# Three pieces of an attention front end: their queries loaded as squares and transposed by VectorE, in place of rows transposed by TensorE

## The chip, the cores and the metric

One core of one Trainium2 chip. The metric is the device time of one execution in us, as the median of several executions. Differences here are of 1 to 5 us in 1028, so means of many runs and 95% intervals matter, and so does each run's mean granted TensorE clock (1.000 is full speed).

## The reference, cut to what matters

```python
scores = scale * np.matmul(q, k.transpose(0, 1, 3, 2))        # q, k, v: (8, 8, 576, 64) fp32
ret    = scores * Dmat                                         # causal, decaying by head
x      = np.matmul(ret, v)  ->  (4608, 512)
h      = x @ w_in                                              # 512 -> 2048
g      = h * erf(softplus(h))
out    = g @ w_out                                             # 2048 -> 512
```

The attention is computed in 36 pieces of 128 tokens. The two large products follow and take nearly all the time.

## The kernel before: the parts concerned

Both operands of the scores have the head dimension on the partitions, so each piece of q and k is transposed. There are two ways to do it. A piece loaded as rows (two DMAs of 128 KB, runs of 256 B) is transposed by TensorE (PE) in four instructions into PSUM, and ScalarE copies it out. A piece loaded as squares of 32 x 32 (four DMAs of 112 KB, runs of 896 B) is transposed in one instruction by VectorE (DVE) into SBUF. Here q is in rows for pieces 0 to 7 and in squares from 8 on.

```python
SQUARES = 2 * PC                 # PC = 4: pieces 0 to 7 of q are rows
...
for name in names:               # load(i, names)
    if name == "q" and i < SQUARES:
        t["q"] = load_rows(i, "q", q, 2)
    elif name == "q":
        t["qs"] = load_squares(i, "q", q)
...
def transposes(i):
    ...
    for name in "qk":
        if name + "s" in t:
            nc.vector.transpose(out=tT..., in_=squares...)              # L322
        else:
            nc.tensor.transpose(pt[:, p, :], ..., ident)  x4            # L328
            nc.scalar.copy(out=tT..., in_=pt...)
    load(i + 2, "q")
def outputs(i):
    ...
    load(i + 3, "kv")
...
# the front part; a: next attention stage, p: next plain product of the first chunk,
# w: load weights, 5: five steps of rounding a weight block on DVE
for what in "alkakakawkakakawaa3awwa2aaa5ppappawwppa5ppapp5wawcppa5ppappaa5s":
```

Where a stage stands in that string fixes what each of its instructions stands behind on its engine. The trace of after shows it: the transpose of piece 6 started on DVE at 51.13 us, right behind the rounding step before it (L271), although its squares had all landed at 43.61.

## Time and profile before

| | before |
|---|---|
| median of 6 runs | 1027.55 us (1027.11 to 1028.71) |
| span of the profiled run, clock | 1026.0 us, 0.999 |
| PE busy | 1017.5 us, 99% |
| DVE busy | 669.1 us, 65%, but 9.46 of 10 us between 40 and 50 us |

PE is the bound over the whole, but before 60 us it works in turn with DVE and the loads. The prediction shows the lines. What is missing there is the list of PE's waits (engine, line, what ended the wait: us in all, times, longest). These are three of its five lines for the kernel before; the other two are 1.4 us at the very start and 0.8 us for a state that GpSimd (POOL) makes:

```profile
PE pt_k L328 <- DMA raw_k<-in_k_dram: 0.7, 2, 0.4
PE p L546 <- DVE wa L271: 0.7, 1, 0.7
PE s L343 <- DVE kT L322: 0.2, 1, 0.2
```

No wait of PE on the changed path reaches 1 us. The trace of before also has what the two ways cost: one of PE's 128x128 transposes takes 273 ns (median), but four, overlapping, take 0.44 us of the chain (46.39 to 46.83); DVE transposes a piece of q of 128x512 in 699 ns (median), 24 times, and ScalarE copies only the eight pieces that are in rows (586 ns each). SyncE's loads take turns on eight semaphores there (100 to 107), each after the landing of the one eight places before: the load of raw_v at 27.40 us was issued right after the one of 20.06 had landed at 27.34.

### The profile page before, as it was taken

To read this page: it belongs to the slowest core of one execution; us is meant where nothing else is said; L and a number is where in the kernel's file an instruction comes from. 1 tells how busy PE (TensorE), PEld (TensorE's weight loads), DVE (VectorE), ACT (ScalarE), POOL (GpSimd) and SP (SyncE) were. 2 spreads that over 40 slices of the span, in tenths; PEclk is the share of its full clock that TensorE was granted. 3 is DMA by queue.
4 is the path that set the end of the run, shared out by engine and by line. 5 is a ranking of instruction groups with operands and counts; after the bars stand their busy time and mean duration, and the time that the engine had idled before them with its cause. 6 is when DMAs were issued, how large, how long until landed. Compare 5 with 4: busy or idle time off the path is not lost.

```text
span 1026.0 us, 15946 instructions
## 1 busy us (share of the span) xinstructions
PE 1017.5 (99%) x6346; PEld 876.1 (85%) x6346; DVE 669.1 (65%) x1054; ACT 390.4 (38%) x481; POOL 123.7 (12%) x122
## 2 busy tenths in 40 slices
PE   9999999999999999999999999999999999999998
PEld 8778888888888888888888888888888888888887
DVE  3868777877976656656666666666567655555555
ACT  2254134233234444434343444444433333333332
POOL 2143112122312110010001001000100000000000
PEclk9999999999999999999999999999999999999999
DMA  9999889979984344544444345444333334444333
GB/s 197 191 241 194 224 194 221 251 155 248 242 187 161 120 150 145 168 158 163 156 150 163 123 146 160 167 144 144 144 124 124 123 131 126 131 136 133 124 91 115
DMA packets 146986, 165.76 MB, mean 162 GB/s; under 512 B 97376, under 2 KB 121568, under 8 KB 138848
## 3 DMA queue, kind: packets, MB, share of 16 engines
q1 hardware_dynamic: 145904, 163.96, 56.5%
q8 instruction: 50, 0.82, 0.3%
q10 hardware_dynamic: 1008, 0.79, 0.3%
q14 instruction: 24, 0.20, 0.1%
HBM read 117.52 MB, written 47.19 MB: 161 GB/s over the span
## 4 chain that ended last, share of the span: by engine, by line
PE 89%; DMA 5%; DVE 3%; SPq 3%; issue 1%; POOL 0%; DVEq 0%; POOLq 0%
PE a L600 23%; PE a L492 22%; PE g L600 11%; PE g L492 11%; PE e L600 6%; PE e L492 5%; PE s L343 3%; PE o L361 2%; DMA raw_qs<-in_q_dram 1%; PE p L546 1%; SPq L145 1%; PE o L384 1%; PE o L372 1%; DMA raw_k<-in_k_dram 1%; SPq L131 1%; DMA raw_ks<-in_k_dram 1%
## 5 line engine op out<-in xcount | busy, mean ns | idle before, releaser
L492 PE MATMUL a<-x,wa 128*128 128x256 f32 x1088 | 258.3, 380 | 0.0
L492 PEld LDWEIGHTS a<-x,wa 128*128 128x128 f32 x1088 | 205.7, 190 | 28.5
L600 PE MATMUL a<-wb,s 128*128 128x256 f32 x864 | 205.7, 381 | 0.0
L600 PEld LDWEIGHTS a<-wb,s 128*128 128x128 f32 x864 | 162.9, 190 | 23.6 <-ACT o L614 0.7
L99 DVE TENSOR_TENSOR t<-g,t 128x512 f32<-128x512 f32 x68 | 46.9, 690 | 150.3 <-ACT t L522 113.1
L492 PE MATMUL g<-x,wa 128*128 128x256 f32 x544 | 129.2, 380 | 0.0
L492 PEld LDWEIGHTS g<-x,wa 128*128 128x128 f32 x544 | 102.8, 190 | 14.4
L99 DVE TENSOR_TENSOR o<-a,o 128x512 f32<-128x512 f32 x108 | 74.2, 687 | 49.3 <-PE a L600 49.3
L517 ACT COPY t<-a 128x512 f32<-128x512 f32 x34 | 19.9, 586 | 188.2 <-PE a L492 188.2
L99 DVE TENSOR_TENSOR t<-t,s 128x1024 f32<-128x1024 f32 x72 | 89.6, 1285 | 0.0
L561 ACT ACTIVATE s<-t 128x1024 f32<-128x1024 f32 x72 | 72.1, 1049 | 27.8 <-DVE t L99 27.8
L270 POOL TENSOR_TENSOR wraw<-wraw 128x512 f32<-128x512 f32 x28 | 29.5, 1053 | 435.6 <-DVE wraw L268 178.9
L99 DVE TENSOR_TENSOR x<-x 128x512 f32<-128x512 f32 x115 | 75.8, 692 | 1.2
L528 ACT COPY t<-a 128x512 f32<-128x512 f32 x34 | 19.9, 587 | 144.4 <-PE a L492 144.4
L565 ACT ACTIVATE s<-s 128x1024 f32<-128x1024 f32 x72 | 72.1, 1049 | 0.4
L600 PE MATMUL g<-wb,s 128*128 128x256 f32 x288 | 68.6, 381 | 0.0
L600 PE MATMUL e<-wb,t 128*128 128x256 f32 x288 | 68.5, 380 | 0.0
L600 PE MATMUL a<-wb,t 128*128 128x256 f32 x288 | 68.5, 380 | 0.0
L600 PE MATMUL g<-wb,t 128*128 128x256 f32 x288 | 68.2, 380 | 0.0
L99 DVE TENSOR_TENSOR sT<-s,cst 128x512 f32<-128x512 f32 x72 | 46.2, 682 | 32.5 <-PE s L343 32.5
L99 DVE TENSOR_TENSOR o<-g,o 128x512 f32<-128x512 f32 x72 | 49.3, 684 | 24.6 <-ACT o L614 19.8
L492 PE MATMUL e<-x,wa 128*128 128x256 f32 x272 | 64.8, 381 | 0.0
(75 smaller groups left out, 1226.2 us busy)
## 6 DMA issues: line engine op xcount, KB each, us to landing
od<-o SPq DMA_DIRECT2D x54, 512.0 KB, 3.3
x<-xd SPq DMA_DIRECT2D x27, 1024.0 KB, 4.8
o<-od SPq DMA_DIRECT2D x27, 1024.0 KB, 5.2
raw_qs<-in_q_dram SPq DMA_DIRECT2D x96, 112.0 KB, 4.4
raw_ks<-in_k_dram SPq DMA_DIRECT2D x84, 112.0 KB, 4.1
xd<-x SPq DMA_DIRECT2D x9, 1024.0 KB, 5.3
raw_k<-in_k_dram SPq DMA_DIRECT2D x64, 128.0 KB, 4.5
raw_v<-in_v_dram SPq DMA_DIRECT2D x64, 128.0 KB, 4.5
```

What stands on the lines that cost most here:

```text
L99: nc.vector.tensor_tensor(out=out, in0=in0, in1=in1, op=op)
L131: nc.sync.dma_start(out=t[part * SQ : (part + 1) * SQ, :, at : at + m - SQ], in_=tokens[:, :, d0 : d0 + m - SQ])
L145: nc.sync.dma_start(out=t[r0 : r0 + n, e::2, :], in_=heads.rearrange("h p d -> p h d"))
L270: engine.tensor_tensor(out=r_f, in0=high_f, in1=r_f, op=ALU.mult)
L343: nc.tensor.matmul(ps[e][:, p, :], lhsT=t["kT"][heads[e], p, :], rhs=t["qT"][heads[e], p, :], start=True, stop=True)
L361: nc.tensor.matmul(o[p % 2][heads[(e + p) % 2], p // 2, :], lhsT=t["v"][:, 2 * p + e, :], rhs=t["sT"][:, e, p, :], start=(p < 2), stop=(no ...
L492: nc.tensor.matmul(acc[:, j * TH : (j + 1) * TH], lhsT=weights["wa", self.g][:, a, d, j * P : (j + 1) * P], rhs=x[self.g, self.c][a][:, d, :],
L517: nc.scalar.copy(out=self.t1[:, 1], in_=self.a)
L528: nc.scalar.copy(out=self.t2[:, 0], in_=self.a)
L561: nc.scalar.activation(self.s[:, j], t, AF.Softplus)
L565: nc.scalar.activation(self.s[:, j], self.s[:, j], AF.Erf)
L600: nc.tensor.matmul(acc[:, tp, :], lhsT=left[:, j * TH + tp * P : j * TH + (tp + 1) * P], rhs=weights["wb", self.g][:, b, j, :], start=(sta ...
```

## The change

Its intent: PE is 99% busy and DVE 65%, so move query transposes from PE to DVE. It does so for pieces 5, 6 and 7 (the sixth to eighth).

```diff
-    SQUARES = 2 * PC
+    SQUARES_Q = PC + 1
...
-                if name == "q" and i < SQUARES:
+                if name == "q" and i < SQUARES_Q:
...
-        if i < SQUARES:
+        if i < 2 * PC:
             weigh_values(i)
...
-        if i + 1 >= SQUARES:
+        if i + 1 >= 2 * PC:
             weigh_values(i + 1)
```

The last two edits keep the scaling of the values where it was.

## The prediction

> **What bounds the kernel now.** I read the page first: the busy times, then the slices. The first number after an engine is its busy time in us, in brackets the share of the span.
>
> ```profile
> PE 1017.5 (99%) x6346; PEld 876.1 (85%) x6346; DVE 669.1 (65%) x1054; ACT 390.4 (38%) x481; POOL 123.7 (12%) x122
> PE   9999999999999999999999999999999999999998
> DVE  3868777877976656656666666666567655555555
> DMA  9999889979984344544444345444333334444333
> ```
>
> TensorE (PE) is the bound nearly everywhere. But the slices show another kernel in front: in the first 60 us DMA and VectorE (DVE) are as full as PE. I therefore asked for busy time by stretch (columns: stretch, its length, then busy us and instructions of each engine, clock, DMA share, GB/s).
>
> ```profile
> 0.00:20.00 20.00, 18.18 (x194) 16.61 (x194) 4.93 (x10) 4.70 (x7) 4.28 (x10) 1.00 0.95 192
> 40.00:60.00 20.00, 18.31 (x197) 14.97 (x196) 15.91 (x30) 11.63 (x19) 5.71 (x6) 1.00 0.87 193
> 40.00:50.00 10.00, 9.28 (x95) 7.51 (x93) 9.46 (x17) 2.85 (x5) 1.80 (x2) 1.00 0.96 206
> 80.00:1020.00 940.00, 939.78 (x5533) 811.51 (x5528) 617.02 (x959) 359.69 (x434) 100.78 (x94) 1.00 0.54 158
> ```
>
> From 80 us on PE idles 940.00 - 939.78 = 0.2 us. So whatever PE loses or gains before 80 us should move the end by as much, and nothing later gives it back. Between 40 and 50 us DVE is at 9.46 of 10: there DVE, not PE, sets the pace. All three changed pieces fall in just this front part: the transposes of their queries on PE start at 31.61, 46.23 and 51.85 us. The chain of waits (start us, us, what) says what PE waits for there:
>
> ```profile
> 26.32 6.20 DMA raw_k<-in_k_dram
> 32.52 0.14 issue
> 32.65 0.63 PE pt_k L328 x4
> ...
> 38.42 1.14 PE s L343 x16
> 39.56 1.27 DVE sT L99 x2
> ...
> 43.65 0.70 DVE wa L271
> 44.35 0.04 issue
> 44.40 1.99 PE p L546 x8
> 46.39 0.44 PE pt_q L328 x4
> 46.83 0.44 PE pt_k L328 x4
> ```
>
> So the path goes from a DMA (keys of the sixth piece, landing at 32.52) through PE to DVE (mask of the scores, then six steps rounding a weight block) and back to PE's first product, which idles 0.72 us for them.
>
> [...]
>
> **The change part by part.**
>
> *Removed from PE:* per piece four transposes, 0.44 us of PE time when their input is there (46.39 to 46.83). Three pieces: 1.3 us, the whole upside. *Removed from ScalarE:* three copies of 0.59 us; ScalarE is at 38% and these are not on the path, so 0.
>
> *Added to DVE:* three transposes of 0.70 us, about 0.65 us each in a dense row; 2.0 us in all, where DVE is full.
>
> *Loads.* Per piece two row DMAs of 128 KB become four square DMAs of 112 KB (448 KB for 256 KB, since the rows overlap). In a dense stream row DMAs land about 0.52 us apart: the two of q and the two of k of the sixth piece are issued at 23.81, 25.22, 25.77 and 26.32 and take 7.14, 6.25, 6.22 and 6.20 us, landing at 30.95, 31.47, 31.99, 32.52. Square DMAs land 0.47 to 0.67 us apart: those issued at 88.75, 89.13, 89.60 and 90.08 take 2.5, 2.6, 2.7 and 2.9 us. I take 0.46 for squares. So per piece 4 x 0.46 - 2 x 0.52 = +0.8 us of DMA time ahead of the keys, in spite of the larger runs. The number of DMAs matters too: each issue waits for the landing of the one eight places before it (the order of instructions shows eight semaphores in rotation), so the keys' DMAs move two places and issue at about 27.4 and 28.4 in place of 25.8 and 26.3. That is still some 5 us before they would land, so I charge nothing for it.
>
> *Moved:* the order of instructions is the point that the diff does not show. On DVE, in order, the sixth piece's transpose stands behind the second weight block's rounding and before the state of the fifth piece: harmless, the squares are there at 32.3 and DVE passes there at about 35. The seventh piece's transpose stands **behind** the last step (L271) of the fourth weight block; the scores of that piece on PE must now wait for it. In before, PE did these scores while DVE was still rounding:
>
> ```profile
> 48.92 1.16 PE L343 MATMUL s<-qT,kT 64*128 64x128 f32 x16
> 49.25 0.69 DVE L271 TENSOR_TENSOR wa<-wa,wraw 128x512 f32<-128x512 f32 x1
> 50.02 1.99 PE L546 MATMUL p<-x,wa 128*128 128x256 f32 x8
> ```
>
> The scores start 1.0 us before L271 ends (49.94) and the products that need L271 follow without a gap. In after it must be L271, transpose, scores, products, one after the other. The eighth piece's transpose comes behind four rounding steps well before its scores: hidden.
>
> *Sum, replayed with the durations above.* Step 1: keys of piece six land at 32.52 + 0.84 = 33.4; their transposes on PE end at 34.1 in place of 33.28: **+0.85**, although the query transposes there are gone (PE simply waits about 1.9 us from 31.55). Everything to L271 of the fourth block moves with it: scores, mask, third block, products at 45.3, fourth block, L271 end at 50.8. The third block's load has 0.85 us of slack of its own (landed 39.13, DVE takes it up at 40.75 because of the mask), and the step before it has moved by the same, so it does not bind. The removed query transposes of piece seven (0.44) only lengthen the wait. Step 2: 50.8 + 0.67 transpose = 51.5; scores 1.09, so the products start at 52.6 in place of 50.02: **another +1.75**. Step 3: piece eight has no query transposes on PE: **-0.44**. Sum +0.85 + 1.75 - 0.44 = +2.2 us. From there to 59.3 us the chain alternates PE and DVE as before and is only shifted, and after that PE is full. 1027.58 + 2.2 = 1029.8.
>
> **Rivals.** (a) *The bound engine simply loses work:* -1.3 us, 1026.3. For it: PE 99% and the engine taking the work at 65%. Against it: those are averages over 1026 us; in the 30 us concerned DVE is at 95% and PE waits. (b) *Larger runs relieve the DMA:* keys arrive earlier. If they landed by 31.6, PE would save about 1.2 us there, and with step 2 and 3 the sum is about 0: 1027.6. For it: [...] 512 packets in place of 1024, and SP's issues being held up to 4.9 us in this stretch with rows. Against: the landing intervals measured above. (c) *The wait moves on:* the extra DMA time of 0.8 us per piece delays a weight block beyond its slack, or later pieces' squares: up to 2 us more, 1031.8. For it: DMA is at 0.87 to 1.05 to 60 us. Against: the seventh and eighth pieces' keys have over 1 us of slack in the replay. (d) *The two new PE gaps (about 1.9 and 2.2 us) cool the clock:* 2 us or more on top; [...] unlikely.
>
> **Range and chances.** The three steps are known to some tenths each; the least sure is step 1 (0 to +1.5), next the length of the fourth block's rounding, which took 4.7 us where the third took 3.6 while GpSimd worked beside it. I hold rival (b) at one in six, (a) at one in twelve, (c) at one in six. That gives 1029.8, with 1027.0 to 1031.6 for 8 in 10. All rivals together stay within 0.5%, and 2% is 20 us, so "within 2%" at 0.985; faster 0.005, slower 0.01 (a slip in the order that I do not see).
>
> **What would show it.** Right: PE's 16 scores of the seventh piece start just after a DVE transpose that starts just after L271 of the fourth block, with a PE gap of about 2 us before them; the keys of the sixth piece land near 33.4 and PE waits for them; PE still full after 80 us; PE busy about 1.3 us less, span 2 us more. Step 1 is wrong if those keys land before 32.5; step 2 if the scores start before L271 ends or the gap is under 1 us. The whole is wrong if PE is idle less than before ahead of 60 us, or if PE shows gaps after 80 us.

## The result, and the profile after

| | before | after |
|---|---|---|
| median of 6 runs | 1027.55 us | 1033.18 us (1030.1 to 1036.5) |
| span of the profiled run, clock | 1026.0 us, 0.999 | 1031.2 us, 0.998 |
| PE busy | 1017.5 us | 1016.9 us |
| DVE busy | 669.1 us | 670.5 us |

The ratio of fast runs is 1.0054 [1.0034, 1.0074]. Ratios here are the mean time of one kernel's fast runs over that of the other's of the same rounds, so not quite the ratio of the medians quoted. By the 2% rule it is "same", but the time lies above the predicted range, and the runs spread over 6 us where those of before spread over 1.6.

The page of after, busy times and three rows of slices:

```profile
PE 1016.9 (99%) x6334; PEld 875.3 (85%) x6334; DVE 670.5 (65%) x1057; ACT 389.1 (38%) x478; POOL 122.6 (12%) x122
PE   8899999999999999999999999999999999999998
DVE  3868877877876666666566666666667655555555
DMA  9997979979984444444445344444433334444333
```

The averages hardly moved, and PE is busy less than before while the kernel is longer. So look at stretches (length, busy us and instructions of PE, PEld, DVE, ACT, POOL, then clock, DMA share, GB/s):

```profile
40.00:60.00 20.00, 17.12 (x147) 13.71 (x148) 14.32 (x25) 6.47 (x11) 5.12 (x5) 0.91 0.98 207
80.00:1020.00 940.00, 938.62 (x5538) 810.34 (x5537) 619.48 (x963) 360.77 (x436) 100.82 (x94) 1.00 0.54 157
```

PE did no more than 17.12 of 20 us there (18.31 before) at a clock of 0.91; after 80 us it idles 1.4 us in 940 (0.2 before). PE's waits in after:

```profile
PE pt_k L328 <- DMA raw_k<-in_k_dram: 2.6, 2, 2.0
PE s L343 <- DVE qT L322: 2.2, 1, 2.2
PE s L343 <- DVE kT L322: 1.4, 1, 1.4
```

The first two are steps 1 and 2 of the prediction, in name and nearly in size. The third lies at 240 us and is taken up below. The chain of waits shows step 2 in full, and one thing more:

```profile
50.52 0.04 DVE wa L271
...
51.13 0.71 DVE qT L322
51.85 0.14 issue
51.98 1.16 PE s L343 x16
53.14 3.40 PE p L546 x8
56.54 0.65 PE pt_k L328 x4
```

The last rounding step, the transpose, the scores and the products now come one after the other, as predicted. But the eight products took 3.40 us; the same eight took 1.99 us at 50.02 in the kernel before (the prediction shows that line). Busy time by windows between the changes of the granted clock tells why (columns as above; third from the end is the clock):

```profile
50.02:53.43 3.41, 1.45 (x18) 1.33 (x19) 2.07 (x4) 1.01 (x2) 0.00 (x0) 1.00 1.00 342
53.43:56.84 3.41, 3.41 (x11) 2.68 (x10) 3.31 (x7) 1.07 (x3) 0.29 (x1) 0.50 0.51 112
56.84:60.25 3.41, 3.41 (x39) 2.75 (x41) 0.19 (x1) 2.80 (x6) 3.04 (x3) 1.00 0.85 242
```

After a window in which PE was busy 1.45 of 3.41 us, the clock was 0.50 for the whole next window, then 1.00 again. Half a window of work is lost: 3.41 x 0.50, about 1.7 us.

To locate gains and losses I compared the start of the same instruction in two traces: of the scores of piece 5 (after step 1), 6 (after step 2) and 7 (after step 3), which the prediction calls the sixth, seventh and eighth piece, and the end. Us later than in the first profile of before:

| profile | clock falls | piece 5 | piece 6 | piece 7 | first output product (84 us) | end |
|---|---|---|---|---|---|---|
| predicted | 0 | +0.85 | +2.6 | +2.2 | +2.2 | +2.2 |
| after, first | 1 | +1.27 | +3.06 | +4.31 | +3.99 | +5.26 |
| before, again (two looks) | 0 | -0.07, +0.44 | -0.07, +0.44 | -0.07, +0.44 | -0.39, +0.13 | +0.64, +0.96 |

All three steps are there, plus a fall of the clock in the products between pieces 6 and 7 (+1.7), plus 1.3 us late. The theory after this: the three steps are right, and the pause that step 2 makes on PE pulls its clock down in some executions, depending on how it lies against windows of 3.41 us; that is the excess and the spread. Rivals: the loads land later than the sum has it; or late waits for key squares have grown.

### The profile page after: what moved, and what is told of

Same layout as the page of the kernel before. It is cut to its first block, busy times and chain, and to the rows that moved or that the text cites. A ratio compares the mean times of both kernels' runs of the same rounds, so it can differ in the third digit from the quotient of the medians.

```text
span 1031.2 us, 15926 instructions
## 1 busy us (share of the span) xinstructions
PE 1016.9 (99%) x6334; PEld 875.3 (85%) x6334; DVE 670.5 (65%) x1057; ACT 389.1 (38%) x478; POOL 122.6 (12%) x122
## 4 chain that ended last, share of the span: by engine, by line
PE 92%; DMA 4%; SPq 2%; DVE 1%; issue 0%; DVEq 0%
PE a L600 24%; PE a L492 22%; PE g L600 12%; PE g L492 11%; PE e L600 6%; PE e L492 6%; PE s L343 3%; PE o L361 3%; PE o L384 1%; PE o L372 1%; DMA raw_k<-in_k_dram 1%; DMA wraw<-in_moe_w_in_dram 1%; DMA raw_qs<-in_q_dram 1%; PE p L546 1%; SPq L145 1%; SPq L131 1%
```

## The experiments

All gave correct results. Edits are against the changed kernel, shortened.

### One piece at a time

```diff
-                if name == "q" and i < SQUARES_Q:
+                if name == "q" and i < 2 * PC and i != 5:     # only_sixth; 6: only_seventh; 7: only_eighth
```

> Only the sixth piece's queries as squares; seventh and eighth as rows. Theory A (the predicted chain, plus a clock that falls when TensorE idles for most of one of the throttle's windows of 3.41 us): step 1 alone. Keys of the sixth piece land about 0.8 us later than in the kernel before, TensorE waits about 2 us for them, the scores of the seventh piece again run before the last rounding step L271 ends. Without a fall of the clock 1028.4 us; runs with a fall 1.0 to 1.7 us more. Rival B (the excess over the prediction comes from later waits for loads, in the stretch of 100 to 300 us, and has nothing to do with the clock): 1028.4 plus 1 to 2 us at a mean clock as before, with a wait of over 1 us after 100 us in the profile.

> Only the seventh piece's queries as squares. Theory A: step 2 alone. The scores of the seventh piece wait for the transpose that waits for L271 of the fourth block: TensorE gap of about 1.6 us (rows of the sixth piece leave TensorE less idle before), products at L271 end + 0.7 + 1.1 us. Without a fall of the clock 1029.3 us, with one 1030.5 to 1031. No long wait for the sixth piece's keys. Rival B: 1029.3 plus 1 to 2 us at an unchanged clock, wait after 100 us.

> Only the eighth piece's queries as squares. Theory A: step 3 alone, four TensorE transposes gone and nothing waits for the VectorE transpose: 1027.1 us, 0.4 below the kernel before; no TensorE gap over 1 us after 5 us, clock as before (0.999), runs within 1 us of each other. If squares cost TensorE by themselves, or DMA time in this stretch binds (rival B), it is at or above the kernel before.

| run | median (range), runs | ratio to before | piece 5 | piece 6 | piece 7 | end | runs with clock 0.998 or less |
|---|---|---|---|---|---|---|---|
| only_sixth | 1029.87 (1027.89 to 1031.94), 13 | 1.0013 [1.0005, 1.0021] | +1.34 | +1.34 | +1.34 | +2.36 | 1 |
| only_seventh | 1031.37 (1029.27 to 1031.94), 10 | 1.0024 [1.0015, 1.0033] | +0.35 | +2.15 | +2.15 | +2.61 | 3 |
| only_eighth | 1028.97 (1027.57 to 1033.93), 14 | 1.0006 [0.9995, 1.0017] | +0.68 | +0.69 | +0.25 | +1.20 | 2 |

(Before on the same chip: 1028.56, 1027.19 to 1030.08, 32 runs, none under 0.999.) Steps 2 and 3 are in the profiles by themselves: 2.15 - 0.35 = +1.80 for the seventh, 0.25 - 0.69 = -0.44 for the eighth. The sixth's +1.34 is not step 1 alone: its piece 4, which the change does not touch, was already at +1.46, and only_seventh and only_eighth, which load piece 5 as rows, are at +0.35 and +0.68. The step is sized below. Against the expectations the times missed upwards: +1.3, +2.4 and +0.7 us over the mean of before, where +0.9, +1.8 (without a fall) and -0.4 were expected. The clock does not account for all of that: the seven runs of only_seventh at 1.000 are 2.2 us above before, on the mean. The sum of the ratios' excesses is 0.43%, close to the 0.44 to 0.54% of the whole. In the profile the eighth's gain is not banked: PE then waits 1.2 us for the keys of the tenth piece.

### Filling the pauses of PE with work that nothing needs

If the clock falls because PE is idle, products of the identity in the pause should keep it up, at no cost as long as they end before the operands come. They are in front of the scores of piece 6 (fill_gap), and in fill_both, fill_little and fill_pair also in front of the key transposes of piece 5.

```diff
     def scores(i):
         ...
+        if i == 6:
+            for _ in range(18):     # fill_both, fill_pair: 8; fill_little: 3
+                nc.tensor.matmul(ps[0][:, 0, :], lhsT=ident, rhs=ident, start=True, stop=True)
     def transposes(i):              # not in fill_gap
         ...
+        if i == 5:
+            for _ in range(8):      # fill_little: 3
+                nc.tensor.matmul(pt[:, 0, :], lhsT=ident, rhs=ident, start=True, stop=True)
```

> The changed kernel with 18 useless transposes' worth of matmuls (identity by identity, into a PSUM place that the scores overwrite) on TensorE just before the seventh piece's scores, where it idled 2.15 us. Theory A: the path is the same, TensorE is merely busy in the gap, so the clock no longer falls: mean clock 0.999 in nearly all runs, 1030.0 to 1031.2 us, spread under 1.5 us (the gap before the sixth piece's keys of 2.0 us is still there, and may let the clock fall in some run). Rival B: no change, 1033 us with runs from 1030 to 1036.

> The changed kernel itself once more, on the chip of the next three runs, for comparison. Theory A (chain of +2.2 us, plus windows of 3.41 us at half the clock that come when TensorE idles for most of one): median 1032 to 1034.5 us, run times falling together with the mean clock, which lies between 0.995 and 0.999. Theory C (the excess over +2.2 is only the unsteady landing of early and later loads, as the 3 us of spread in the kernel before on this kind of chip would suggest): the same times, but unrelated to the clock.

> The changed kernel with 8 useless products of the identity (0.23 us each at fp32, as the earlier filling run showed: 18 took 4.18 us, too long for the gap) in each of the two TensorE gaps: before the sixth piece's key transposes and before the seventh piece's scores. About 1.9 us of filling for gaps of 2.0 and 2.15 us. Theory A: mean clock 0.999 to 1.0 in all runs, median 1030 to 1031.3 us, no run over 1033. Theory C: median as that of the changed kernel in this call, within 0.5 us.

> The changed kernel with only 3 useless products (0.7 us) at the start of each of the two TensorE gaps, which leaves gaps of about 1.3 and 1.4 us. Theory A, sharpened: in the ten profiles so far the clock fell after those windows of its 3.41 us grid in which TensorE idled 1.97 and 2.01 us, and after none with 1.73 us or less. So two gaps under 1.5 us cannot lower it: clock 0.999 to 1.0 in all runs, 1030 to 1031.5 us, as with the longer filling. If instead any gap of over 1 us can do it, the clock is 0.998 or less in half of the runs and the median 1032 to 1033.

fill_gap missed: 1034.39 (1031.51 to 1038.26, 6 runs), ratio 1.0065 [1.005, 1.008], slower than the change itself. The 18 products took 4.18 us for a pause of 2.2, so the scores started late by the difference, and three of six runs still were at 0.998 or less. The other pause, before the keys of piece 5, had been left open; that it is the reason is not shown, since none of the three was profiled. With both pauses filled and fewer products:

| run | median (range), runs | ratio to before | clocks of the runs |
|---|---|---|---|
| after_again | 1032.42 (1030.09 to 1033.32), 5 | 1.0044 [1.0031, 1.0057] | 1.000, 0.998 x3, 0.997 |
| fill_both, same chip | 1030.91 (1030.0 to 1032.39), 5 | 1.0032 [1.002, 1.0045] | 1.000 x3, 0.999 x2 |
| fill_little, another chip | 1031.5 (1029.53 to 1034.05), 13 | 1.0029 [1.0021, 1.0038] | 1.000 x8, 0.999 x5 |

No run of these filled kernels fell under 0.999, which shows that the pauses pull the clock down. It does not settle the times: at clocks of 0.999 or 1.000 fill_both is still 3.2 us and fill_little 2.9 us above the mean of before, and the 13 runs of fill_little spread over 4.5 us. Three products in each pause were enough to hold the clock at 0.999 or more in all 13 runs; PE's timeline of fill_little (start us, us, what, in brackets the wait):

```profile
49.79 0.83 PE L346 MATMUL s<-ident 128*128 128x128 f32 x6
52.11 1.16 PE L349 MATMUL s<-qT,kT 64*128 64x128 f32 x16 [1.49 <-DVE qT L322]
53.20 1.99 PE L552 MATMUL p<-x,wa 128*128 128x256 f32 x8
```

(The three products are six records.) The pause is cut from 2.2 to 1.49 us and the eight products take 1.99 us. The time gained is 1.2 us on the means of the pair on one chip, with overlapping intervals, so it was tried again at the end (below).

### Taking away the cause of each step

transpose_early moves the transpose of piece 6 ahead of the fourth weight block's rounding; early_and_keys_first also loads the keys of pieces 5 to 7 before their queries.

```diff
-    for what in "...ppapp5wawcppa5...":
+    for what in "...ppappe5wawcppa5...":       # e: early_q(6), DVE's transpose of the loaded squares
```
```diff
-        load(i + 2, "q")                        # in transposes
+        if i + 2 not in (5, 6, 7):
+            load(i + 2, "q")
...
-        load(i + 3, "kv")                       # in outputs
+        if i + 3 in (5, 6, 7): load k, then q, then v of i + 3
+        else: load(i + 3, "kv")
```

> The changed kernel with the seventh piece's VectorE transpose put ahead of the fourth block's rounding, the only change. Step 2 of the chain then costs 0.65 us (the transpose itself on VectorE) in place of 1.75: the scores run beside the rounding again, TensorE waits for L271 with its products for about 0.6 us. With step 1 +0.85 and step 3 -0.44: +1.1 us over the kernel before. Theory A: one of the two long gaps is gone, so fewer falls of the clock: in all +1.1 to +2.5 us. If step 2 was not the cause, it is as slow as the changed kernel.

> The same, and the keys of the sixth to eighth piece are loaded ahead of their squares of queries. Step 1 then falls away: the sixth piece's keys land at about 31.9 us, their transposes on TensorE start without a long wait, and the whole runs at -0.8 (step 1 turned round) + 0.65 - 0.44 = -0.6 us: at or up to 1 us below the kernel before, no TensorE gap over 1.2 us, clock as in the kernel before, so no slow runs. If squares bind by their DMA time itself and not by standing ahead of the keys, it is no faster than the run with the early transpose alone.

transpose_early: 1029.66 (1028.7 to 1032.33, 8 runs), ratio 1.0024 [1.0013, 1.0034]. Its timeline has the old order again:

```profile
49.09 1.16 PE L351 MATMUL s<-qT,kT 64*128 64x128 f32 x16
50.13 0.69 DVE L271 TENSOR_TENSOR wa<-wa,wraw 128x512 f32<-128x512 f32 x1
50.88 1.99 PE L554 MATMUL p<-x,wa 128*128 128x256 f32 x8 [0.62 <-DVE wa L271]
```

The scores start before the rounding ends, piece 6 is at +0.17, where the five profiles of the changed kernel have +2.33 to +4.59, and the end at +0.95. That settles step 2's cause. Two of eight runs still were at 0.998; the first pause was still there.

early_and_keys_first missed: 1031.19 (1029.48 to 1034.92, 9 runs), ratio 1.0035 [1.0022, 1.0048], where a gain was expected. In its profile pieces 6 and 7 did start 1.07 and 0.84 us *earlier* than in before. That gain was lost twice: 1.4 us in a wait for the tenth piece's keys, and later PE waited 2.5 us for key squares and its clock fell at 237.94 us, after a window with 2.01 us idle. The likely reading is that loads moved ahead push other loads back; for the tenth piece's keys the next runs bear it out, for the wait near 240 us nothing tests it.

### Can the eighth's gain be banked?

The keys of the tenth piece are put ahead of its queries, with only the eighth piece changed (eighth_keys_ahead), without any change (before_keys_ahead, an edit of the kernel before), and together with all of the above (all_ahead). As in the edit above, transposes then leaves those queries out.

```diff
+        if i + 3 in (9,): load k, then q, then v      # all_ahead: (5, 6, 7, 9), and early_q(6)
```

> Only the eighth piece as squares, and the tenth piece's keys loaded ahead of its query squares. Theory A': the 0.44 us of step 3 were lost again at the tenth piece, whose keys TensorE then waited for (1.2 us in the profile of the run with the eighth piece alone). With those keys about 2 us earlier the gain stays: 0.3 to 0.5 us below the kernel before, if the run below of the order alone gains nothing. Rival: the saving is lost elsewhere, same as the kernel before.

> The kernel before with the tenth piece's keys loaded ahead of its query squares, the only change: separates the order from the squares. TensorE reaches that place at about the moment when the keys land (67.86 and 67.84 us), so at most 0.1 to 0.3 us faster; same within noise.

> The changed kernel with the early VectorE transpose of the seventh piece, the keys of the sixth to eighth piece ahead of their squares, and the tenth piece's keys ahead too. The run without the last part was 0.84 us ahead of the kernel before at 64 us and lost 1.4 us to the tenth piece's keys. Now that wait is gone: first product of the second half of the block at 83.6 to 84.0 us in place of 84.49, and with clocks of 1.0 about 0.5 to 0.8 us below the kernel before in the middle of its runs. If the loads as a whole bind (squares take more DMA time than rows), the wait moves to the next load and it is no faster than the kernel before.

| run | median (range), runs | ratio to before |
|---|---|---|
| eighth_keys_ahead | 1029.05 (1027.79 to 1030.58), 13 | 1.0003 [0.9995, 1.0011] |
| before_keys_ahead | 1028.28 (1027.67 to 1030.54), 13 | 0.9998 [0.999, 1.0007] |
| all_ahead | 1031.26 (1029.53 to 1033.2), 13 | 1.0022 [1.0014, 1.0031] |

In the profile of eighth_keys_ahead the wait for the tenth piece's keys is gone and the first output product starts 0.21 us earlier than in the first profile of before. But two other profiles of before lie at -0.39 and +0.13 there, and the times show no gain. all_ahead missed: its front is level with before (+0.04 at 84 us), yet it ends +3.0 us late, with 2.4 us of waits for key squares. No version tried beats the kernel before.

### Two more looks at each kernel

> The kernel before, one more profile. Asked: how long TensorE waits for the key squares (VectorE's transpose of them) between 205 and 285 us, 0.2 us in its first profile. Theory D (the change makes this late wait longer): 0 to 0.5 us here and 0.5 to 2.6 in the profiles of the changed kernel. Theory E (it is unsteady landing that both share): 0 to 1.5 us in both. No window with over 1.5 us of TensorE idle, no fall of the clock.

> The kernel before, as in the first look: theory D 0 to 0.5 us of late wait, theory E 0 to 1.5 us; no fall of the clock.

> The changed kernel, one more profile. Theory D: late wait 0.5 to 2.6 us. Theory E: 0 to 1.5 as in the kernel before. For the clock: a fall to half for 3.41 us comes after each window of the grid with over about 1.9 us of TensorE idle and after none with under 1.7; up to 53 us the delay is +2.2 us plus 1.7 for each fall.

> The changed kernel, as in its first look: theory D 0.5 to 2.6 us of late wait, theory E 0 to 1.5 us; falls of the clock after windows with over about 1.9 us of TensorE idle and no others.

Single runs (state unknown) on one chip: before 1028.38 and 1028.74, after 1035.39 (clock 0.997) and 1030.36 (clock 1.000). The late waits for key squares were 0.8 and 0.9 us in before, 2.1 and 1.1 us in after: before missed theory D's 0 to 0.5, and 2.1 is over theory E's 1.5, so neither stands as it was put. The rule for the clock held: at piece 7 after_look1, with two falls, is at +5.84 us (2.2 + 2 x 1.7 = 5.6 expected), after_look2, with none, at +1.89 (2.2). The two profiles of after are the same program, 5.0 us apart, and show the cause best. The pause before the scores of piece 6 in the good one, PE's timeline:

```profile
51.26 1.16 PE L343 MATMUL s<-qT,kT 64*128 64x128 f32 x16 [2.20 <-DVE qT L322]
52.35 1.99 PE L546 MATMUL p<-x,wa 128*128 128x256 f32 x8
```

and its two clock windows around it:

```profile
49.70:53.11 3.41, 1.85 (x20) 1.69 (x21) 2.06 (x5) 1.23 (x2) 0.00 (x0) 1.00 1.10 317
53.11:56.52 3.41, 3.41 (x20) 2.75 (x20) 3.10 (x7) 2.25 (x4) 0.69 (x1) 1.00 0.71 106
```

The pause is the same 2.2 us as in the first profile of after (2.15), but a boundary at 49.70 cuts it, so the window holds 1.56 us of idling and the clock stays. In the bad one both pauses lie within a window, and both are followed by half speed:

```profile
30.89:34.30 3.41, 1.09 (x8) 0.72 (x7) 2.66 (x5) 1.07 (x2) 0.00 (x0) 1.00 0.86 170
34.30:37.72 3.42, 3.42 (x9) 2.25 (x8) 1.32 (x3) 0.59 (x1) 1.04 (x1) 0.50 0.77 192
51.37:54.78 3.41, 1.27 (x17) 1.18 (x18) 2.06 (x4) 1.23 (x2) 0.00 (x0) 1.00 0.96 235
54.78:58.19 3.41, 3.41 (x9) 2.59 (x10) 3.31 (x7) 0.58 (x1) 0.11 (x1) 0.50 0.81 206
```

### The pair once more

> The changed kernel once more, five rounds, on the same chip and in the same call as fill_pair. Theory (the pause pulls TensorE's clock down in most executions): most of its runs have a mean clock of 0.998 or less, those are at 1032 to 1036 us, and the runs at 0.999 or 1.0 are at 1030 to 1030.5; mean about 1032.5. Rival (the excess over the predicted +2.2 us is late loads, not the clock): the times do not sort by the clock.

> The changed kernel with 8 identity products in each of the two pauses, once more, on the same chip as after_pair. Theory: no run under 0.999, and the mean is 1 to 2 us under that of after_pair, near 1031, since the three serial steps (+2.2 us) and 0.2 us of products that overrun stay. Rival: same mean as after_pair within 0.5 us, since the work is the same and the products do nothing.

On one chip in one call (before 1028.33, 11 runs): after_pair 1033.52 (1030.97 to 1035.86, 6 runs), ratio 1.0052 [1.0038, 1.0065]; fill_pair 1032.36 (1031.46 to 1032.58, 5 runs), ratio 1.0039 [1.0027, 1.0051]. Five of the six runs of after_pair were at 0.998 or 0.997 and took 1032.85 or more; the one at 0.999 took 1030.97. No run of fill_pair was under 0.999. Its mean is 1.25 us lower, as in the first pair (1.2), again with overlapping intervals, and not quite near 1031: in its profile the keys of piece 5 landed only at 34.35 us (33.84 in the first profile of after), and the products of the identity held PE from 32.85 to 34.63 us, some 0.3 us past that, so that the scores of piece 5 were 1.95 us late. A fixed filling does not fit a pause whose length varies.

The 17 timed fast runs of the changed kernel (first result, after_again, after_pair) sort by the clock:

| mean clock of the run | runs | mean us | range |
|---|---|---|---|
| 0.999 or 1.000 | 3 | 1030.39 | 1030.09 to 1030.97 |
| 0.998 | 10 | 1033.25 | 1032.16 to 1034.22 |
| 0.997 or less | 4 | 1034.32 | 1031.92 to 1036.5 |

All three runs at 0.999 or more are faster than all the others. Below that the order is loose: the runs of 1031.92 and 1033.01 at 0.997 are faster than most at 0.998. One fall of 3.41 us at half speed takes 0.0017 off the mean clock.

## Why the prediction was wrong

It said 1029.8 with 1031.6 as the upper end, and 1033.18 was measured.

**Step 1 was right in kind and near in size.** +0.85 was predicted. In five profiles of the changed kernel the scores of piece 5 are +1.27, +0.90, +2.80, +0.49 and +1.58 late; the third includes a clock fall of 1.7, so +1.1 without it. The mean of the five is +1.07. But the first profile of before is among the earliest at this place: the six other profiles in which piece 5 is still in rows lie between -0.07 and +1.12, so that the step itself is nearer +0.6 (an estimate: 1.04, the mean of the five and of only_sixth and transpose_early, less 0.44, the mean of the seven with rows). The keys' landing shows it best. The second key load of piece 5 landed at 33.84 in the first profile (33.4 predicted), and at 33.06 to 34.14 in the five, against 32.45 to 33.20 in the seven with rows. In the first profile it stood behind four squares that landed 0.50 to 0.65 us apart, not 0.46.

**Step 2 was right.** +1.75 was predicted; from piece 5 to piece 6 the five profiles lose 1.79, 1.79, 1.79, 1.84 and 1.79. transpose_early removed the wait and piece 6 was at +0.17.

**Step 3 was right up to piece 7.** -0.44 was predicted; the two profiles of after without a fall at this place have -0.44 and -0.44, and so has only_eighth.

**The sum was right for runs whose clock did not fall.** In these two profiles piece 7 is at +2.25 and +1.89, and the end at +2.35 and +2.62. The three timed runs at 0.999 or more are 2.3 to 2.6 us above the mean of before in the same submission; +2.2 was predicted. With step 1 at +0.6 the three steps measure about +1.95, so some of this agreement is luck: up to 0.6 us of it comes from elsewhere, such as the late waits below.

**What failed is the dismissal of rival (d).** The prediction itself named two new pauses of about 1.9 and 2.2 us; they came out at 2.0 and 2.2 in the first profile (over all five the first of them was between 0.7 and 2.3, the second always about 2.2). It called a fall of the clock unlikely, with no measurement of this case behind it. But the falls came with just such pauses. I laid a grid of 3.41 us from the clock's own records over all 20 profiles of this study, leaving out the start and the last 4 us, and added up PE's idle time in each window. That the records keep to such a grid is seen in the first two profiles: in after they start at 5.64, 53.43, 56.84 and 1029.64 us, which is 14, 1 and 285 times 3.413 us apart, in before at 7.33 and 1024.51, 298 times. The five falls follow windows with 1.97, 2.01, 2.14, 2.16 and 2.32 us idle. No window with 1.73 us or less was followed by one, and none lies between. So in these traces the windows with a fall after them and those without part somewhere between 1.73 and 1.97 us idle, and a pause of 2.2 us comes out on the side of a fall only if no boundary cuts it well inside. As an estimate, with the parting put at 1.85 us, between those two numbers, and the grid at random, that is so in (2 x (3.41 - 1.85) - (3.41 - 2.2)) / 3.41 = 0.56 of executions. Three of the five profiles have a fall at this pause, and 3 of the 10 runs of only_seventh, which has this pause alone, are at 0.998. Hence a large part of the spread between runs, which I had put nowhere in the range; not all of it, since fill_little spreads over 4.5 us without a fall. Where the grid lies differs from run to run: a boundary stood at 50.02 us in the first profile of after, at 51.37 in after_look1 and at 49.70 in after_look2. Half speed lasted one window, from 53.43 to 56.84 us in the first. In the first profile of before no window between 7.33 and 1021 us holds more than 0.72 us of idling and the clock is 1.00 up to 1024.51, so that trace could not have told what a pause of 2 us does.

**Its size.** The mean clocks of the 17 runs are on average 0.0021 under 1, which is 0.0021 x 1030 = 2.2 us; the runs of before whose clocks are listed in two of the three submissions are 0.0001 and 0.0004 under 1 themselves, which leaves about 1.9 us for the pauses. The mean excess over before is 4.4 to 5.5 us in the three submissions (ratios 1.0044, 1.0052, 1.0054), so the steps (2.0 to 2.2) and the clock (1.9) leave 0.3 to 1.6 us. The table of the 17 runs says the same: those at 0.998 are 2.9 us above those at 0.999 or more, and one fall costs 1.7. Filling the pauses keeps the clock up but gave back only 1.2 us in each pair (both pairs taken together, 1.2 us with a standard error of 0.5, an estimate from the runs' scatter). The filled runs had other delays: late loads, and some 0.3 us of overrun in the one profile looked at. So the cause is shown for the clock, for the time only to that extent.

**Rival (c) in part.** The rest is in waits for the key squares near 240 us, together with small ones to 285 us: between pieces 24 and 32 the five profiles of after lose 1.18, 0.32, 2.03, 0.95 and 0.95 us more than the first of before. But before itself lost 1.03 and 0.84 in its two other profiles. Whether the change lengthens these waits is open: the two groups overlap. Such a wait can also pull the clock down, as early_and_keys_first shows at 237.94 us; that may be what two runs of only_eighth at 0.998 and 0.996 had, but none of these was profiled.

**Rivals (a) and (b)** fell as predicted: PE's own work was not what counted in the front, and larger runs did not bring the loads forward. In this dense stretch the four squares of piece 5 in after, 112 KB each in runs of 896 B, landed 0.50 to 0.65 us apart, and the rows in before, 128 KB each in runs of 256 B, 0.52 us apart. Other loads share the DMA engines there (DMA share 1.06 from 28 to 35 us in after), so this does not test the length of the runs by itself.

**Its own signs, and a misreading.** One sign of "the whole is wrong" came true: PE shows gaps after 80 us (1.4 us idle in 940, in the wait near 240 us; the two other profiles of before have 0.8 and 0.9 us of it too). And DVE is at 95% only between 40 and 50 us; over the 30 us that the prediction argues with (30 to 60 us) it is busy 22.6 us, 75%. Rival (a) fell for where the transpose stands, not for a DVE full throughout.

## What to carry to other kernels

An engine's share of the whole span does not tell what a move to or from it is worth: here the "free" engine was at 9.46 of 10 us just where the work was put, and its instruction landed behind a rounding step and ahead of scores that had been done in its shadow. Before a change opens a pause on TensorE, lay it against the length of the clock window of the trace: here a pause of about 2 us in a window of 3.41 us was followed by a fall to 0.50 in three of five profiles, and cost 1.7 us more on top of itself. When the same kernel's runs spread over several us, sort them by mean clock first, and then see what spread is left.
